# Moving the loads of one batch to a later point of the GpSimd queue, and a batch's sums ahead of a group of h, in a fused convolution and mixer kernel

## Chip, cores and metric

The kernel runs on one core of a Trainium2 chip. The metric is the device time of one execution in microseconds; the time of a kernel is the median of several runs. A change of under about 1% is hard to tell from no change with it.

## What is computed

The input x has 8 batches of 4224 tokens with 192 channels, in float32. First comes a causal convolution with 7 taps; each of 8 heads (24 channels each) has its own taps, which are softmaxed. Its result, here called y, goes through a mixer: a low-rank mix over the tokens (rank 32) gives h, and then come two matrix products over the channels with a ReLU between them.

```python
w = softmax(weight, axis=-1)                       # 8 heads x 7 taps
out = np.einsum('hk,bskhg->bshg', w, x_unf)        # causal windows of 7 tokens
x = out.reshape(B, S, D)                           # this is y below
xt = x.transpose(0, 2, 1)
h = xt @ U @ V                                     # U: 4224x32, V: 32x4224
u = x + h.transpose(0, 2, 1)
ch = np.maximum(u @ w_ch1, 0.0) @ w_ch2            # 192 -> 768 -> 192
return (u + ch).astype(np.float32)
```

## The kernel before

**Tiles and groups.** A tile is 128 tokens. A batch has 33 tiles, and the 264 tiles of all batches are taken in 33 groups of 8, so that a group may lie across two batches.

**Convolution.** The x of a batch is loaded into `x_sb` (two buffers, so that batches b and b + 2 share one), as bf16, in blocks of 64 tokens on half of the partitions each. `x_part` (L76) is one load of a part of it, issued on the GpSimd (POOL) queue; the list `XP` (L84) has the four parts of a batch: two of 384 KB, one of 432 KB and one of 408 KB. From batch 2 on, the convolution (`conv32`, matmuls at L340, results moved to `y_sb` at L272 on ScalarE and at L274 on VectorE) also needs `xb_sb`, a rearranged copy of `x_sb` with a single buffer. `x_shift` (L299) makes it with four GpSimd copies: L303, L304 and twice L316. Between these copies it also loads the batch that comes next: after L304 it clears the halo of the next `x_sb` (L74) and issues the first two parts, and after the copies of L316 the other two, all at L79. The condition for that, `more`, is in L308.

**Mixer.** The sum of y times U over the tokens of a batch is `tt_mm` (33 matmuls at L399). `tt_split` takes it out of PSUM as a high part (ScalarE, L413) and a low part (VectorE, L414), and `tt_sum` adds these up with two matmuls at L455 and writes `tt_sb` (VectorE, L449). For a group g, `h_group` multiplies `tt_sb` by V (8 matmuls at L484) and adds y on VectorE (L506), which gives `u_sb`. `transp` (L523) has SP issue a DMA transpose of `u_sb` to `uT` (L525). `w1` multiplies `uT` by W1 (36 matmuls of 512 columns at L578, six blocks m of six) and applies the ReLU on ScalarE (L589) or VectorE (L591). `w2` multiplies that by W2 for two tiles at a time (12 matmuls at L602), VectorE adds u (L610, tile `out_sb`, eight buffers), and SP issues the store (L617). The transposes and the stores share one hardware DMA queue; the loads of x go through the software queue that GpSimd serves. PSUM has eight banks, given out in turn by `bank()`.

**Order.** The schedule is manual: every engine executes its instructions in the order in which the program emits them, and the order is written out by hand in `SLOTS` (L630). A slot first does W1 of its groups and then W2 of its groups, with four places p per group; at a place, other work is put in ahead of W2: `h` and a number is `h_group` and `transp` of that group, `c` a piece of the convolution (batch, first head, number of heads, engines that move it out), `x` is `x_shift`, `t` is `tt_mm` and `tt_split`, and `s` is `tt_sum`. The slots that matter here:

- slot 2: W1 of group 2, W2 of group 1; at place 4 h of group 4 and `x2`
- slot 3: W1 of group 3, W2 of group 2; at place 1 h of group 5
- slot 4: W1 of groups 4 and 5 one after the other, W2 of groups 3, 4 and 5; at places 0, 4, 7 and 10 h of groups 6, 7, 8 and 9, at places 1 to 3 the convolution of batch 2, and at place 3 `x3` behind it
- slot 5: W1 and W2 of groups 6 to 8; the convolution of batch 3 begins at place 3, and `x4` is at place 7
- slots 6 to 9 (k = 6 to 9 in the loop of L651): W1 and W2 of three groups each; the convolution of batch b = k - 2 at places 4, 5 and 8, with `x{b+1}` behind its last piece, the third h of the slot and `t{b}` at place 10, and `s{b}` at place 12, behind the slot's last W2

**Held loads.** For batch 2 alone, `LOADS` (L682) puts the loads elsewhere: each of the four parts is emitted behind the W1 of a group and waits for the end of one of its six blocks (`held`, L619; the pair (2, 5) is the last block of W1 of group 2). The loop at L737 does this for every batch that `LOADS` names.

Of the kernel before, what the change touches and what calls it, by code (L numbers as in the profile page):

```python
# [14 lines left out]
def kernel(  # L15
# [12 lines left out]
    B, S, D = x.shape  # L28
# [33 lines left out]
    xt = [None] * B  # L62
# [7 lines left out]
    def x_tile(b):  # L70
        xt[b] = xs.tile([P, NB1 + 1, D], BF16, name="x_sb")

    def x_zero(b, eng):
        eng.memzero(xt[b][0:HB, 0, :])  # L74

    def x_part(b, r, s0, s1):  # L76

        blk = NB0 * r + s0 - 1
        return nc.gpsimd.dma_start(  # L79
            out=xt[b][HB * r : HB * r + HB, s0:s1, :],  # L80
            in_=x[b, blk * HB : (blk + s1 - s0) * HB, :].rearrange("(j p) d -> p j d", p=HB),
        )

    XP = [(0, 1, 17), (0, 17, NB0 + 1), (1, 0, 18), (1, 18, NB1 + 1)]  # L84
# [214 lines left out]
    def x_shift(b):  # L299


        xbt[b] = xbs.tile([P, NB1, D], BF16, name="xb_sb")
        nc.gpsimd.tensor_copy(out=xbt[b][:, 0:NB0, :], in_=xt[b][:, 1 : NB0 + 1, :])  # L303
        nc.gpsimd.tensor_copy(  # L304
            out=xbt[b][HB : HB + QB, NB0:NB1, :],
            in_=xt[b][HB : HB + QB, NB0 + 1 : NB1 + 1, :],
        )
        more = XP if b + 1 < B and xt[b + 1] is None else []  # L308
        if more:
            x_tile(b + 1)  # L310
            x_zero(b + 1, nc.gpsimd)
        for xp in more[:2]:
            x_part(b + 1, *xp)
        for r in range(2):
            q = slice(HB * r + QB, HB * r + HB)
            nc.gpsimd.tensor_copy(  # L316
                out=xbt[b][q, 0 : (NB0, NB1)[r], :], in_=xt[b][q, 0 : (NB0, NB1)[r], :]
            )
        for xp in more[2:]:
            x_part(b + 1, *xp)  # L320
# [249 lines left out]
    def w1(g, pat):  # L570
        rl = rls.tile([P, MC, 2, 4 * P], BF16, name="rl_sb")
        rlt[g] = rl
        ends = []
        for m in range(MC):
            pp = [bank(), bank()]
            for c in range(3):
                for hf in range(2):
                    last = nc.tensor.matmul(  # L578
                        out=pp[hf][:],
                        lhsT=W1_sb[HB * hf : HB * hf + HB, c, m * P : (m + 1) * P],  # L580
                        rhs=uTt[g][HB * hf : HB * hf + HB, :, c, :],
                        start=(c == 0),
                        stop=(c == 2),
                        tile_position=(HB * hf, 0),
                    )
            ends.append(last)
            for hf in range(2):
                if pat[m][hf] == "A":
                    nc.scalar.activation(out=rl[:, m, hf, :], in_=pp[hf][:], func=ACT.Relu)  # L589
                else:  # L590
                    nc.vector.tensor_scalar_max(out=rl[:, m, hf, :], in0=pp[hf][:], scalar1=0.0)  # L591
        return ends
# [58 lines left out]
    for k in range(5, 14):  # L651
        gs = list(range(3 * k - 9, 3 * k - 6))
        hs = [f"h{g}" for g in range(nh, min(nh + 3, NG))] + [None] * 3
        nh = min(nh + 3, NG)
        if k == 5:
            at = {
                0: [hs[0]],
                3: ["c3:0:3:A"],
                4: ["c3:3:2:AAD"],
                5: [hs[1]],  # L660
                7: ["c3:5:3:AD", "x4"],
                9: ["t3"],
                10: ["s3"],
                11: [hs[2]],
            }
        elif k < 10:
            b = k - 2
            at = {
                0: [hs[0]],
                4: [f"c{b}:0:3:AAD"],  # L670
                5: [f"c{b}:3:3:AAD"],
                6: [hs[1]],
                8: [f"c{b}:6:2:AD"] + ([f"x{b + 1}"] if b + 1 < B else []),
                10: [hs[2], f"t{b}"],
                12: [f"s{b}"],
            }
        else:
            at = {0: [hs[0]], 4: [hs[1]], 8: [hs[2]]}
        SLOTS.append((gs, gs, {p: [w for w in what if w] for p, what in at.items()}))
    assert nh == NG  # L680

    LOADS = {2: [(1, 5), (1, 5), (2, 2), (2, 5)]}  # L682


    idle(30, P)
# [27 lines left out]
    def do(what):  # L713
        if what[0] == "c":
            b, h0, n, engs = what[1:].split(":")
            conv32(int(b), int(h0), int(n), engs)
            return
        if what[0] == "d":
            for h in range(H):
                conv(int(what[1:]), h, 1, [0, 1], "AD")  # L720
            return
        n = int(what[1:])
        if what[0] == "h":
            h_group(n)
            if n > 1:
                transp(n)
        elif what[0] == "x":
            x_shift(n)
        elif what[0] == "t":
            tt_split(n, tt_mm(n, range(NT)))  # L730
        else:
            tt_sum(n)

    for gs1, gs2, at in SLOTS:
        for g in gs1:
            ends = w1(g, RELU0 if g < 2 else RELU)
            for b, blocks in LOADS.items():  # L737
                for q, (gb, m) in enumerate(blocks):
# [49 lines left out]
```

## Time and profile before

| | |
|---|---|
| median of 5 runs | 336.06 us (333.69 to 337.11) |
| time of the profiled execution | 336.06 us |
| its span, from the first to the last instruction | 334.3 us |
| mean granted TensorE clock | 0.992 |
| busy PE / DVE / ACT / POOL | 319.9 / 274.9 / 166.6 / 139.3 us |
| DMA: software queue (loads of x) / hardware queue (stores, transposes) | 14.73 / 38.18 MB |

The profiled execution lay at the median, and its time is 1.8 us above its span. PE is the TensorE matmul, PEld the weight load beside it, DVE is VectorE, ACT ScalarE, POOL GpSimd, and SP the engine that issues the stores and transposes. Times in the rows are microseconds from the start of the span, and a number behind a line number in a row ("x36") counts instructions. In a row of waits the last three figures are the sum in microseconds, how often, and the longest. "Landing" is the time from the start of the issue of a DMA to its completion.

### The profile page before, as it was taken

Reading aid. Unit: us, or ns where it says so; the run is one execution under the profiler, and the core shown is the slowest. Engines: PE = TensorE matmul, PEld = TensorE weight load, DVE = VectorE, ACT = ScalarE, POOL = GpSimd, SP = SyncE. Lnnn points to the kernel's source line nnn. Section 1 sums busy time; section 2 is a strip of 40 time slices with the busy share of each in tenths; the row PEclk is TensorE's granted clock in tenths of the full one; section 3 lists DMA queues with packets and bytes.
Section 4 is the critical chain, followed back from the end, with each engine's and each line's share of the span. In section 5 each row is a group of like instructions: output and inputs, shape, how many; then the busy total and the mean of one; then the engine's idle time right before and its main releaser. Section 6 shows DMA issues by size and latency. Waiting matters only on the chain.

```text
span 334.3 us, 9715 instructions
## 1 busy us (share of the span) xinstructions
PE 319.9 (96%) x4072; PEld 218.3 (65%) x4072; DVE 274.9 (82%) x558; ACT 166.6 (50%) x340; POOL 139.3 (42%) x91
## 2 busy tenths in 40 slices
PE   6889999789999999999999998999999999999994
PEld 6645676447747846764874784587487487487494
DVE  5746998779988898998898869889798898896863
ACT  1648454463295184558429535842921921912910
POOL 8580217964990796299289529700000000000000
PEclk9989999999999999999999999999999999999998
DMA  8999995969999996998999699077149349249045
GB/s 102 192 166 139 169 212 143 159 121 218 194 220 183 253 148 86 261 202 122 130 288 184 79 248 229 2 190 187 53 82 247 100 111 226 91 109 259 14 129 157
DMA packets 122909, 53.55 MB, mean 160 GB/s; under 512 B 87760, under 2 KB 122832, under 8 KB 122864
## 3 DMA queue, kind: packets, MB, share of 16 engines
q1 hardware_dynamic: 84672, 38.18, 50.1%
q0 software_dynamic: 38192, 14.73, 39.0%
q8 instruction: 32, 0.52, 0.6%
q14 instruction: 13, 0.11, 0.1%
HBM read 29.49 MB, written 25.95 MB: 166 GB/s over the span
## 4 chain that ended last, share of the span: by engine, by line
PE 86%; DMA 5%; DVE 4%; ACT 2%; issue 1%; POOL 0%; SPq 0%; DVEq 0%; POOLq 0%
PE ps L602 39%; PE ps L578 37%; PE ps L340 3%; DMA x_sb<-in_x_dram 3%; PE ps L484 3%; DMA uT<-u_sb 2%; PE ps L399 2%; DVE y_sb L274 2%; ACT y_sb L272 1%; DVE u_sb L506 1%; ACT rl_sb L589 1%; DVE rl_sb L591 1%; PE ps L536 0%; PE ps L369 0%; PE ps L455 0%
## 5 line engine op out<-in xcount | busy, mean ns | idle before, releaser
L589 ACT ACTIVATE rl_sb<-ps 128x512 bf16<-128x512 f32 x235 | 125.4, 603 | 89.2 <-PE ps L578 85.8
L602 PE MATMUL ps<-W_sb,rl_sb 128*128 128x192 bf16 x1584 | 140.5, 246 | 0.8 <-DVE out_sb L610 0.6
L578 PE MATMUL ps<-uT,W_sb 64*128 64x512 bf16 x1188 | 133.4, 380 | 3.6 <-DMA uT<-u_sb 2.9
L602 PEld LDWEIGHTS <-rl_sb 128*128 128x128 bf16 x1584 | 128.3, 98 | 12.1 <-issue 11.5
L591 DVE TENSOR_SCALAR rl_sb<-ps 128x512 bf16<-128x512 f32 x161 | 105.8, 690 | 26.1 <-PE ps L578 25.4
L578 PEld LDWEIGHTS <-W_sb 64*128 64x128 bf16 x1188 | 58.3, 95 | 75.5 <-issue 7.0
L610 DVE TENSOR_TENSOR out_sb<-ps,u_sb 128x384 f32<-128x384 f32 (+1 forms) x133 | 70.0, 550 | 19.5 <-PE ps L602 18.5
L506 DVE TENSOR_TENSOR u_sb<-y_sb,ps 128x192 bf16<-128x192 bf16 (+1 forms) x168 | 66.3, 462 | 0.0
L316 POOL COPY xb_sb<-x_sb 32x6144 bf16<-32x6144 bf16 (+1 forms) x12 | 65.5, 5460 | 0.6
L303 POOL COPY xb_sb<-x_sb 128x6144 bf16<-128x6144 bf16 x6 | 31.8, 5302 | 52.8 <-PE ps L340 27.5
L272 ACT ACTIVATE y_sb<-ps 128x384 bf16<-128x384 f32 (+3 forms) x79 | 32.3, 502 | 36.4 <-PE ps L340 34.6
L79 POOL DMA_DIRECT2D x_sb<-in_x_dram x32 | 27.0, 853 | 17.3 <-PE ps L484 9.6
L274 DVE CAST y_sb<-ps 128x408 bf16<-128x408 f32 (+2 forms) x53 | 26.6, 554 | 2.5 <-PE ps L369 2.5
L484 PE MATMUL ps<-tt_sb,V_sb 32*128 32x192 bf16 x264 | 13.2, 247 | 0.3 <-DVE y_sb L274 0.2
L340 PE MATMUL ps<-xb_sb,band 64*32 64x384 bf16 x192 | 12.4, 332 | 0.1
L340 PE MATMUL ps<-x_sb,band 64*32 64x384 bf16 x192 | 12.1, 332 | 0.0
L484 PEld LDWEIGHTS <-V_sb 32*128 32x128 bf16 x264 | 4.9, 92 | 9.5 <-issue 9.5
L413 ACT ACTIVATE tt_hi<-ps 128x192 bf16<-128x192 f32 x7 | 2.3, 331 | 15.9 <-PE ps L399 15.9
L173 PE MATMUL ps<-zz 128*128 128x128 bf16 x90 | 7.1, 254 | 1.2 <-DVE zz L168 1.2
L173 PEld LDWEIGHTS <-zz 128*128 128x128 bf16 x90 | 6.8, 117 | 1.2 <-DVE zz L168 1.2
L369 PE MATMUL ps<-x_sb,band 64*64 64x312 bf16 (+3 forms) x192 | 7.2, 277 | 0.4 <-DMA x_sb<-in_x_dram 0.4
L340 PEld LDWEIGHTS <-band 64*32 64x32 bf16 x384 | 4.4, 89 | 4.5 <-issue 3.0
(64 smaller groups left out, 71.7 us busy)
## 6 DMA issues: line engine op xcount, KB each, us to landing
out_dram<-out_sb SPq DMA_DIRECT2D x131, 192.0 KB, 3.0
x_sb<-in_x_dram POOLq DMA_DIRECT2D x14, 384.0 KB, 8.0
x_sb<-in_x_dram POOLq DMA_DIRECT2D x7, 432.0 KB, 6.5
x_sb<-in_x_dram POOLq DMA_DIRECT2D x7, 408.0 KB, 8.6
x_sb<-in_x_dram POOLq DMA_DIRECT2D x1, 648.0 KB, 9.7
x_sb<-in_x_dram POOLq DMA_DIRECT2D x1, 624.0 KB, 7.2
uT<-u_sb SPq DMA_TRANSPOSE x31, 5.3
W_sb<-in_moe_w_ch_dram POOLq DMA_DIRECT2D x2, 192.0 KB, 5.8
```

Of the source, the lines that this page charges most:

```text
L272: nc.scalar.activation(out=out, in_=in_, func=ACT.Copy)
L274: nc.vector.tensor_copy(out=out, in_=in_)
L303: nc.gpsimd.tensor_copy(out=xbt[b][:, 0:NB0, :], in_=xt[b][:, 1 : NB0 + 1, :])
L316: nc.gpsimd.tensor_copy(out=xbt[b][q, 0 : (NB0, NB1)[r], :], in_=xt[b][q, 0 : (NB0, NB1)[r], :])
L340: nc.tensor.matmul(out=pp[r][QB * cg : QB * cg + QB, 0 : nk[r] * GS], lhsT=w[hr], rhs=t[hr, st : st + 2 * nk[r] - 1 : 2, hs], start=True, ...
L484: nc.tensor.matmul(out=banks[pr][:, a * D : (a + 1) * D], lhsT=V_sb[32 * q : 32 * q + 32, (j // 8) * 2 + j % 2, :], rhs=ttb[b][32 * q : 32 ...
L506: nc.vector.tensor_tensor(out=u_group(g)[:, i : i + n, :, hf, :], in0=yt[b][:, run[0] : run[0] + n, :].rearrange("p n (c k) -> p n c k", c=3),
L578: last = nc.tensor.matmul(out=pp[hf][:], lhsT=W1_sb[HB * hf : HB * hf + HB, c, m * P : (m + 1) * P], rhs=uTt[g][HB * hf : HB * hf + HB, :, ...
L589: nc.scalar.activation(out=rl[:, m, hf, :], in_=pp[hf][:], func=ACT.Relu)
L591: nc.vector.tensor_scalar_max(out=rl[:, m, hf, :], in0=pp[hf][:], scalar1=0.0)
L602: nc.tensor.matmul(out=cps[:, a * D : (a + 1) * D], lhsT=rlt[g][:, m, hf, (i + a) * P : (i + a + 1) * P], rhs=W2_sb[:, m, :], start=(m == ...
L610: nc.vector.tensor_tensor(out=o[:, 0:n, :].rearrange("p n (c k) -> p n c k", c=3), in0=cps[:, 0 : n * D].rearrange("p (n c k) -> p n c k", ...
```

## The change

Three lines change. With the first, `x_shift(2)` no longer loads batch 3; `x_shift` of batches 3 to 6 loads the next batch as before. With the third, the four loads of batch 3 are emitted behind W1 of groups 4 and 5 and wait for the blocks 1 and 4 of each. On the GpSimd queue they so stand behind all the copies of `x2`, and ahead of those of `x3`; the clearing of the halo goes with the first. With the second, `t{b}` is emitted ahead of the third h at place 10 of slots 6 to 9 (batches 4 to 7), on every engine.

```diff
@@ -305,7 +305,7 @@
             out=xbt[b][HB : HB + QB, NB0:NB1, :],
             in_=xt[b][HB : HB + QB, NB0 + 1 : NB1 + 1, :],
         )
-        more = XP if b + 1 < B and xt[b + 1] is None else []
+        more = XP if 2 < b < B - 1 else []
         if more:
             x_tile(b + 1)
             x_zero(b + 1, nc.gpsimd)
@@ -671,7 +671,7 @@
                 5: [f"c{b}:3:3:AAD"],
                 6: [hs[1]],
                 8: [f"c{b}:6:2:AD"] + ([f"x{b + 1}"] if b + 1 < B else []),
-                10: [hs[2], f"t{b}"],
+                10: [f"t{b}", hs[2]],
                 12: [f"s{b}"],
             }
         else:
@@ -679,7 +679,7 @@
-    LOADS = {2: [(1, 5), (1, 5), (2, 2), (2, 5)]}
+    LOADS = {2: [(1, 5), (1, 5), (2, 2), (2, 5)], 3: [(4, 1), (4, 4), (5, 1), (5, 4)]}
```

## The prediction

> **What bounds it now.** I read the page's busy times first, then TensorE's own waits, then the chain of work that ended last. TensorE is the bound, and what it can still give is small.
>
> ```profile
> PE 319.9 (96%) x4072; PEld 218.3 (65%) x4072; DVE 274.9 (82%) x558; ACT 166.6 (50%) x340; POOL 139.3 (42%) x91
> ```
>
> The waits of TensorE name two that this change touches: one for a transpose and one for the low part of a batch's sum, with a wait for VectorE's `out_sb` just ahead of the latter.
>
> ```profile
> PE ps L578 <- DMA uT<-u_sb: 2.9, 1, 2.9
> PE ps L455 <- DVE tt_lo L414: 1.0, 1, 1.0
> PE ps L602 <- DVE out_sb L610: 0.6, 1, 0.6
> ```
>
> In the chain the first stands as a transfer of 7.45 us between h and W1 of group 5 (W1 of group 4 had ended at 64.75, so TensorE stood for 2.9):
>
> ```profile
> 58.90 1.09 DVE u_sb L506 x3
> ...
> 60.14 7.45 DMA uT<-u_sb
> ...
> 67.64 4.06 PE ps L578 x36
> ```
>
> Why is this transpose slow? The DMA view of two stretches of its life (packets, MB, share) answers: first from 61 to 65 us, then from 65 to 67.6. q0 carries the loads of x, q1 transposes and stores.
>
> ```profile
> q0 software_dynamic: 1761, 0.67, 148.1%
> q1 hardware_dynamic: 11, 0.00, 0.5%
> ```
>
> ```profile
> q1 hardware_dynamic: 1845, 0.60, 107.1%
> q0 software_dynamic: 186, 0.07, 21.5%
> ```
>
> The transpose moves nothing until the two loads of batch 3, issued just ahead of it, are through (the second landed at 66.5). GpSimd's timeline shows these loads (L79 at 58.26) and what stands around them:
>
> ```profile
> 52.22 5.30 POOL L303 COPY xb_sb<-x_sb 128x6144 bf16<-128x6144 bf16 x1 [8.12 <-DMA x_sb<-in_x_dram]
> 57.58 0.50 POOL L304 COPY xb_sb<-x_sb 32x384 bf16<-32x384 bf16 x1
> 58.14 0.17 POOL L74 MEMSET x_sb<- 64x96 uint32 x1
> 58.26 1.63 POOL L79 DMA_DIRECT2D x_sb<-in_x_dram  x2
> 59.93 10.98 POOL L316 COPY xb_sb<-x_sb 32x6144 bf16<-32x6144 bf16 x2
> 70.86 1.72 POOL L79 DMA_DIRECT2D x_sb<-in_x_dram  x2
> 79.83 5.30 POOL L303 COPY xb_sb<-x_sb 128x6144 bf16<-128x6144 bf16 x1 [7.25 <-DMA x_sb<-in_x_dram]
> ...
> 87.54 10.98 POOL L316 COPY xb_sb<-x_sb 32x6144 bf16<-32x6144 bf16 x2
> ```
>
> **Part 1, the loads: what is removed.** Without the loads, the transpose of 60.14 has the DMA engines to itself. The transpose at 226.12, with no load near, landed after 3.7 us; that at 54.23, also without one, after 5.3. So it lands between 63.8 and 65.5, against a W1 of group 5 that can begin at 64.75: TensorE gains 2.1 to 2.9. I take 2.9, since nine of the eleven transposes behind 210 us, where there are no loads left, took 4.0 or less.
>
> **Part 1: what moves.** On the POOL queue the halo and two issues leave the middle of batch 2's copies, so L316 starts at 58.1 and ends at 69.1 instead of 70.9. The convolution of batch 2, which needs them, began at 73.26 and would now begin at 70.4: 1.3 us of room, no cost. Then come the halo and four issues at 0.85 each (1.63 and 1.72 a pair), the first at 69.3, the last at 71.8. Their added waits, for blocks 1 and 4 of W1 of groups 4 and 5, cost nothing: a block takes 11.76 / 18 = 0.65 us (the chain's W1 of three groups), and block 4 of group 5 ends near 68.1. Even if the transpose stayed late, it would end at 70.9, ahead of the fourth issue. Behind these on POOL stand only the copies of batch 3, which have to wait for the landing anyway. SP's queue is not reordered, but its stores and transposes now meet these loads.
>
> **When do they land?** Before, two parts issued at 70.86 let L303 start at 79.83, 8.97 later. Now two parts of 384 KB more are in the same string, 2048 packets. From 23 to 29 us the loads of batch 1 ran alone at 2998 packets in 6 us, or 500 per us; from 61 to 65 it was 1761 in 4 us, or 440. So they add 4.1 to 4.7 us, and L303 of batch 3 starts at 69.3 + 8.97 + 4.1 to 4.7 = 82.4 to 83.0. A second way: the four loads of batch 1, issued together from 18.81, had the last landed at 32.43, 13.6 later: 82.9. L303 so starts some 3 us later than before.
>
> **What is late next.** From L303 to the end of the second L316 it is 98.52 - 79.83 = 18.7 us, whatever else happens. The convolution of batch 3 began at 104.19; with the 2.9 gained TensorE asks for it at 101.3. L303 must then start by 101.3 - 18.8 = 82.5. This is the narrow place of the change: each microsecond later than 82.5 is taken off the gain, and at 85.4 it is gone.
>
> **Rule against row.** The group 6 transpose (issued at 74.59, now near 71.7) falls into the string of four loads. At 60.14 and 131.83, with loads issued about 2 us ahead, the loads went through first. The Trainium skill, DMA: Bandwidth & Descriptors, "Queues, rings and completion order", says otherwise: each DMA engine alternates between the queues that have work, packet by packet. Then the loads would be slowed by everything on q1: a transpose of some 2.2 us (65.4 to 67.6) and the four stores of the first places of W2, 0.5 each by the spacing of their landings: 4.2. L303 would start at 86.6 to 87.2 and the convolution of batch 3 at 105.7, 1.5 later than before: a loss instead of a gain. The row says 0 to 0.6 of the 2.9 is lost. Sharing is seen where the transpose came before the loads or within 1.2 us of them (issued at 85.83: its loads took 8.7 and 11.4 to land). I stay near the row, with 0.5 for a little sharing: L303 at 83.1, the convolution at 101.9, **gain 2.3** (ends: -1.5 and 2.9).
>
> Behind it the chain recovers: loads of batch 4 issued 3.3 later end near 110.5 against a convolution of batch 3 that ends near 108.3, so the POOL copies of batch 4 start about as before (110.77), and the convolution of batch 4 has 4.2 us of room (129.5 to 133.56), 1.9 after the gain. But the second pair of batch 4's loads (98.47, now near 101.8) comes to lie on the transpose of group 10 (103.48, now 101.2). Such a meeting at 187.06 and 188.04 made the stores late, and TensorE lost 0.6 + 1.0; at 158.76 and 159.91 nothing. **I take -0.3** (0 to -1.7).
>
> **Part 2, the order of t and h.** VectorE's timeline at the one place where the low part was late:
>
> ```profile
> 200.53 0.56 DVE L610 TENSOR_TENSOR out_sb<-ps,u_sb 128x384 f32<-128x384 f32 x1 [1.70 <-PE ps L602]
> 201.01 2.07 DVE L506 TENSOR_TENSOR u_sb<-y_sb,ps 128x192 bf16<-128x192 bf16 x6
> 202.99 0.35 DVE L414 TENSOR_TENSOR tt_lo<-ps,tt_hi 128x192 bf16<-128x192 f32 x1
> 203.26 1.01 DVE L610 TENSOR_TENSOR out_sb<-ps,u_sb 128x384 f32<-128x384 f32 x2
> ```
>
> The stores were behind (the wait of 1.70 can only be for a free `out_sb`, as W2 had long ended), and six adds of h stood ahead of the low part. With the new order it runs at 201.0, and the 1.0 goes; the 0.6 stays. Given back: W1's first ReLU on VectorE now follows W1's start by about 2.3 us instead of 0.9; the banks of W2's last pair and of the sum come free near 204.3 and 204.8, and W1's fourth block, which needs them, begins at 202.4 + 3 x 0.65 = 204.4: 0.35 is lost. **Net 0.65** (0 to 1.0). At the other three places TensorE did not wait for the low part. There VectorE will idle 0.65 (the row at 113.96, where no h stands between, waits that long for the high part), its ReLUs come 0.75 later, and PSUM has about 0.2 to 0.3 to spare; I take 0 (0 to -0.3 each). The h moved back is for a W1 a whole slot later, some 28 us.
>
> **Sum.** 2.3 - 0.3 + 0.65 = 2.65 from the profiled execution's 336.06, which is also the median: **333.4**.
>
> **Rivals.** (a) All of it comes: 2.9 + 1.0 = 3.9, so 332.2. For it: the loads of batch 1 and a landing at 82.4. Against: the four loads have never met a transpose. (b) The loads share the DMA engines, and the copies of batch 3 become the bound. The meeting at 187.06 had its pair landed 11.4 after the first issue, the quiet pair at 70.86 took 8.8; at twice the difference, 5.2, for two pairs, L303 starts at 87.9 and the convolution of batch 3 at 106.7, 2.5 later than before; with part 2's 0.65 that is 337.9. It decides against the change from L303 at 86.1 on. Against it is the row at 60.14. (c) Group 5's transpose is no earlier, because the stores or its own work held it, or another stall takes the gain at once: 336. Against it: 11 packets in 4 us.
>
> **How the numbers follow.** Forecast 0.52 (333.4, by itself 332.3 to 334.8), (a) 0.20, (b) 0.19, (c) 0.09. About 1% is what a measurement of this kernel can tell from no change: 332.7 and 339.4. Below 332.7 lie most of (a) and a tenth of the forecast, 0.26; above 339.4 somewhat under half of (b), 0.09, where L303 starts past 89.4; the rest is 0.65. The range reaches from (a) to (b), 331.6 to 338.2.
>
> **What would show it.** Right: no wait of L578 for `uT` near 65 us; L79 four times from 69.3 on; L303 of batch 3 near 83; no idle of TensorE ahead of L340 near 102; no wait of L455. Wrong: a TensorE wait for `xb_sb` there or for group 6's `uT` near 86; new waits for `out_sb`; POOL standing in L79 on W1.

## The result, and the profile after

The changed kernel is slower: 339.34 us median of 43 runs against 336.72 of 80 runs of the kernel before, ratio 1.0092 (95% interval 1.0071 to 1.0114). The ratio compares fast runs alone, those at most 1.5% above the fastest of their kernel, and comes to 3.1 us of loss; the medians differ by 2.6. A gain of 2.65 us was forecast. The runs of either kernel spread over more than 7 us, and the profiled execution of the changed kernel was one of its fastest: 335.83 us, span 334.1. A second profile of it (the tenth experiment) has a span of 339.4. The spans can't be set directly against that of before, since the profiled execution of before lost 1.4 us at its start (TensorE's clock was at half from 22.0 to 25.4 us), where the change can't matter. So I compare stage by stage.

The page of the changed kernel has TensorE as the bound as before:

```profile
PE 321.3 (96%) x4072; PEld 221.3 (66%) x4072; DVE 274.0 (82%) x558; ACT 166.5 (50%) x340; POOL 139.5 (42%) x91
```

The waits of TensorE on the changed kernel, in the first profile and then in the second:

```profile
PE ps L340 <- POOL xb_sb L316: 2.8, 1, 2.8
...
PE ps L578 <- DVE out_sb L610: 0.2, 1, 0.2
PE ps L602 <- DVE out_sb L610: 0.2, 1, 0.2
```

```profile
PE ps L340 <- POOL xb_sb L316: 4.6, 2, 2.6
PE ps L578 <- DVE out_sb L610: 1.2, 2, 0.8
...
PE ps L602 <- DVE out_sb L610: 0.8, 2, 0.6
```

The wait for the transpose of group 5 (2.9) and that for the low part of the sum (1.0) are gone. VectorE's timeline has the low part ahead of the adds of h, right behind the store wait:

```profile
201.63 0.56 DVE L610 TENSOR_TENSOR out_sb<-ps,u_sb 128x384 f32<-128x384 f32 x1 [1.23 <-DMA out_dram<-out_sb]
202.10 0.35 DVE L414 TENSOR_TENSOR tt_lo<-ps,tt_hi 128x192 bf16<-128x192 f32 x1
202.37 2.06 DVE L506 TENSOR_TENSOR u_sb<-y_sb,ps 128x192 bf16<-128x192 bf16 x6
```

A wait for the copies of batch 3 stands in the place of the two, and in the second profile another one at batch 5. GpSimd's timeline of the changed kernel shows where it comes from:

```profile
56.44 10.98 POOL L316 COPY xb_sb<-x_sb 32x6144 bf16<-32x6144 bf16 x2
67.48 0.17 POOL L74 MEMSET x_sb<- 64x96 uint32 x1
67.60 3.35 POOL L79 DMA_DIRECT2D x_sb<-in_x_dram  x4
85.42 5.30 POOL L303 COPY xb_sb<-x_sb 128x6144 bf16<-128x6144 bf16 x1 [14.47 <-DMA x_sb<-in_x_dram]
...
93.15 10.98 POOL L316 COPY xb_sb<-x_sb 32x6144 bf16<-32x6144 bf16 x2
```

The four loads are issued where they should be, but L303 starts 17.8 us after the first of them, not 13.8. The views of the DMA issues give the fourth load 15.2 us to land and the transpose of group 6, issued at 70.08, 12.2. Three stretches of the DMA view tell why, first 71 to 74 us, then 75 to 79, then 79.6 to 80.8 (q0 carries the loads, q1 transposes and stores):

```profile
q0 software_dynamic: 1391, 0.53, 152.6%
```

```profile
q0 software_dynamic: 1122, 0.42, 85.2%
q1 hardware_dynamic: 1104, 0.28, 53.4%
```

```profile
q1 hardware_dynamic: 71, 0.02, 82.0%
q0 software_dynamic: 71, 0.03, 61.5%
```

Up to 74.5 the loads have the engines to themselves, at 464 packets per us. Then the transpose begins, and the two queues move as many packets each: 1122 against 1104. The loads go on at 280 per us. By these rates, five microseconds of sharing cost the loads about 2.0 of the 4.0 us, an estimate. The third stretch is close to a standstill of both queues, for about 1.2 us. The second profile and several experiments have it as well, and the fourth experiment, without this transpose, does not (500 packets in the same stretch); its cause isn't shown. From 81 on the loads share with the stores.

The chain of the changed kernel, in the stretch that follows:

```profile
74.37 10.04 DMA out_dram<-out_sb
...
84.53 0.56 DVE out_sb L610
...
93.15 5.29 POOL xb_sb L316
98.44 0.06 issue
98.50 5.63 POOL xb_sb L316
104.14 0.04 issue
104.18 0.71 PE ps L340 x17
```

A store behind that transpose takes 10 us, VectorE has no free `out_sb` until it lands, and further on the chain lies on GpSimd's copies. From the first W1 of slot 5 to that of slot 6 it is 28.2 us before (89.0 to 117.2) and 34.2 after (84.5 to 118.7). The gain up to slot 5 was made: from W1 of group 4 to W1 of group 6 it is 28.3 before (60.7 to 89.0) and 25.3 after (59.3 to 84.5). The loss of 6.0 in slot 5 is more than the wait of 2.8. W1 of groups 6 to 8 ends 13.3 us after its start instead of 11.8, for want of banks behind the late stores: 1.5. The wait behind it is shorter by as much, since the copies end when they end. And the granted clock, in the view of windows (the column behind the five engines' busy times), falls behind the wait:

```profile
101.00:104.20 3.20, 0.43 (x10) 0.11 (x8) 0.78 (x2) 0.00 (x0) 3.20 (x2) 1.00 1.16 211
104.20:105.00 0.80, 0.80 (x26) 0.43 (x26) 0.00 (x0) 0.41 (x2) 0.80 (x2) 1.00 1.09 365
105.00:108.50 3.50, 3.50 (x35) 2.42 (x34) 1.11 (x2) 3.32 (x9) 0.81 (x1) 0.51 1.14 153
108.50:112.00 3.50, 3.50 (x63) 2.70 (x61) 2.86 (x7) 0.22 (x2) 0.00 (x0) 1.00 1.45 222
```

For 3.4 us of the stretch from 105.0 to 108.5 the clock is at half, which is worth 1.7 us. 2.8 + 1.5 + 1.7 = 6.0, against 3.0 gained: at the start of slot 6 the changed kernel is 2.9 us late. This is not yet the loss of the whole execution. Slot 8, where the profile of before had its waits of 0.6 and 1.0, takes 28.4 us instead of 30.0, so that from W1 of group 4 to the last W1 this execution loses 1.4 us. The second profile loses 6.8: 3.7 up to the start of slot 6, the rest behind it, above all in slot 7 (32.1 us instead of 28.2). That the first profile is 2.9 late at slot 6 and the runs lose 3.1 is a coincidence.

Could the loss be nothing but executions with more half-clock stretches? Of the changed kernel's 44 runs, 18 had a mean clock from 0.9925 to 0.997, median 337.3 us, and 22 a lower one, 341.1. Of the 43 runs of the kernel before that ran beside the fifteenth experiment, 23 lay in the same band, median 336.1, and 13 below it, 337.7. So the loss is there at equal clock too, and low clocks are somewhat more frequent besides.

### The profile page after: what moved, and what is told of

It reads as the page before. It is cut to its first block, busy times and chain, and to the rows that moved or that the text cites. A ratio compares the mean times of both kernels' runs of the same rounds, so it can differ in the third digit from the quotient of the medians.

```text
span 334.1 us, 9716 instructions
## 1 busy us (share of the span) xinstructions
PE 321.3 (96%) x4072; PEld 221.3 (66%) x4072; DVE 274.0 (82%) x558; ACT 166.5 (50%) x340; POOL 139.5 (42%) x91
## 4 chain that ended last, share of the span: by engine, by line
PE 75%; DMA 9%; POOL 6%; DVE 5%; ACT 3%; issue 1%; DVEq 0%; POOLq 0%
PE ps L602 34%; PE ps L578 34%; DMA out_dram<-out_sb 6%; POOL xb_sb L316 3%; DMA x_sb<-in_x_dram 3%; ACT rl_sb L589 2%; PE ps L484 2%; PE ps L340 2%; DVE y_sb L274 2%; POOL x_sb L79 1%; PE ps L399 1%; DVE rl_sb L591 1%; DVE out_sb L610 1%; DVE u_sb L506 1%; DMA V_sb<-in_moe_V_dram 1%
## 5 line engine op out<-in xcount | busy, mean ns | idle before, releaser
L602 PEld LDWEIGHTS <-rl_sb 128*128 128x128 bf16 x1584 | 129.2, 98 | 12.1 <-issue 11.4
L578 PEld LDWEIGHTS <-W_sb 64*128 64x128 bf16 x1188 | 59.7, 94 | 69.9 <-issue 6.5
L610 DVE TENSOR_TENSOR out_sb<-ps,u_sb 128x384 f32<-128x384 f32 (+1 forms) x133 | 69.8, 550 | 25.4 <-PE ps L602 21.6
L303 POOL COPY xb_sb<-x_sb 128x6144 bf16<-128x6144 bf16 x6 | 31.8, 5302 | 55.8 <-DMA x_sb<-in_x_dram 32.3
L340 PE MATMUL ps<-xb_sb,band 64*32 64x384 bf16 (+1 forms) x192 | 13.1, 340 | 2.9 <-POOL xb_sb L316 2.8
```

What stands on the lines that cost most here:

```text
L340: nc.tensor.matmul(out=pp[r][QB * cg : QB * cg + QB, 0 : nk[r] * GS], lhsT=w[hr], rhs=t[hr, st : st + 2 * nk[r] - 1 : 2, hs], start=True, ...
L578: last = nc.tensor.matmul(out=pp[hf][:], lhsT=W1_sb[HB * hf : HB * hf + HB, c, m * P : (m + 1) * P], rhs=uTt[g][HB * hf : HB * hf + HB, :, ...
L602: nc.tensor.matmul(out=cps[:, a * D : (a + 1) * D], lhsT=rlt[g][:, m, hf, (i + a) * P : (i + a + 1) * P], rhs=W2_sb[:, m, :], start=(m == ...
L610: nc.vector.tensor_tensor(out=o[:, 0:n, :].rearrange("p n (c k) -> p n c k", c=3), in0=cps[:, 0 : n * D].rearrange("p (n c k) -> p n c k", ...
```

## The experiments

Fifteen kernels were run, and the changed kernel once more. Theory 1: the loss is in the string of four loads that meets the transpose of group 6. Its first rivals: the new order of t and h costs (theory 2 of the first two expectations); any later load only moves the collision (rival 3); four loads in a string are slow by themselves (rival 4). From the eleventh experiment on, theory 2 is a new one, given before it. Ratios are to the kernel before, with 95% intervals.

### Each part alone

The first experiment has the changed lines 308 and 682 alone, the second line 674 alone.

> The loads of batch 3 moved, the order of t and h as before. Theory 1 (the loss lies in the moved loads: four loads in one string meet the transpose of group 6, the DMA engines are shared, the copies of batch 3 end late and the stores fall behind): 0.6 to 1.2% slower, about what the whole change gave; TensorE waits about 2 to 4 us for xb_sb ahead of the convolution of batch 3, and L303 of batch 3 starts some 17 to 18 us after the first of the four loads. Theory 2 (the loss lies in the new order of t and h, which makes VectorE's ReLUs late): faster by 0 to 0.7%.

> The sums of a batch ahead of h, the loads as before. Theory 1 (the loss lies in the moved loads): within 0.3% of before, at most 0.3% faster, and no TensorE wait of L455 for the low part at any of the four places. Theory 2 (the new order makes VectorE's ReLUs late): 0.6 to 1.2% slower, with TensorE waiting for banks in the W1 behind each of the four sums.

Loads alone: 1.0168 (1.0126 to 1.021). Order alone: 0.9987 (0.9963 to 1.0012). The loss is in the loads, and larger than the 0.6 to 1.2% expected; theory 2 of these two falls. The two ratios don't multiply to the 1.0092 of the whole change: beside the moved loads the new order seems worth more than by itself, which was not followed up. With the loads alone TensorE waited 3.7 us for the copies, and L303 started 18.6 us after the first load. With the order alone the wait of L455 is not in the profile, which leaves the one for the transpose:

```profile
PE ps L578 <- DMA uT<-u_sb: 3.4, 1, 3.4
```

### Another place for the first pair

Third experiment, from the kernel before:

```diff
-        for xp in more[:2]:
+        for xp in more[:2] if b > 2 else []:
             x_part(b + 1, *xp)
         for r in range(2):
             ...
+            for xp in more[:2] if (b, r) == (2, 0) else []:
+                x_part(b + 1, *xp)
```

> As before, but the first pair of batch 3's loads is issued between the two copies of L316, some 5.5 us later than before and behind the issue of the transpose of group 5; the second pair stays behind the second copy. Theory 1 (the gain at group 5 is real, and it was lost since all four loads went into one string with the transpose of group 6): the transpose of group 5 lands in 3.7 to 4.5 us, TensorE does not wait for it, the copies of batch 3 end before TensorE asks, and the kernel is 0.5 to 0.9% faster. Rival 3 (any later load of batch 3 makes later transfers collide and gives the gain back): within 0.3% of before.

The transpose of group 5 landed in 3.65 us and TensorE did not wait for it. But eight of nine runs took 336.7 to 340.3 us and one 329.6, so that no ratio is given; faster it is not, and as a forecast of theory 1 this missed. The profile shows four waits for `xb_sb`, 6.0 us in all. The transpose of group 6 came earlier with the gain, at 69.96, and so between the issues of the second pair (69.37 and 70.20), whose last part took 13.3 us to land. The collision had moved, as rival 3 has it.

### The transpose left out

Fourth experiment, from the whole change:

```diff
-            if n > 1:
+            if n == 6:
+                uTt[n] = uTt[n - 1]
+            elif n > 1:
                 transp(n)
```

> The whole change, but the transpose of group 6 is left out, and W1 of group 6 reads the transposed tile of group 5 instead; everything else is done. Theory 1 (the transpose shares the DMA engines with the four loads): the loads run alone for longer and L303 of batch 3 starts 2 to 3 us sooner than with the whole change, 15 to 15.5 us after the first load (what is left of sharing is with the stores), TensorE's wait for xb_sb falls to about 0 to 1 us, and the stores are no longer late; 0.7 to 1.2% faster than the whole change, about level with before. Rival 4 (four loads in a string are slow by themselves, by the descriptors or the memory): L303 starts no sooner than 17 us after the first load, and the time stays within 0.3% of the whole change.

Ratio 1.0005 (0.9982 to 1.0029): level with before, as theory 1 expected, but not by its path. L303 still started 16.6 us after the first load (15 to 15.5 was expected, 17 or more by rival 4), as the next transpose and the stores took the left-out one's share, and TensorE still waited for the copies:

```profile
PE ps L340 <- POOL xb_sb L316: 3.4, 1, 3.4
```

Slot 5 took 34.2 us as with the whole change, and the four slots behind it 28.0 to 28.3 each. So the traffic of the other queue matters, not this one transpose; and what the profiles have to tell this kernel from the second one of the whole change lies in the slots behind slot 5. Rival 4 gets no support: the four loads of batch 1, with nothing on the other queue until the last of them was through, landed in 13.6 us, and the string takes longer where other traffic meets it.

### The transpose of group 6 later

In these four h of group 6 stands at place 2 of slot 4 instead of place 0:

```diff
-                0: ["h6"],
                 1: ["c2:0:3:AAD"],
-                2: ["c2:3:3:AD"],
+                2: ["c2:3:3:AD", "h6"],
```

> The first pair of batch 3's loads between the copies of L316, as in the third experiment, and h of group 6 with its transpose moved from place 0 to place 2 of slot 4, so that the transpose is issued some 3 to 4 us after the second pair. Theory 1 (a transpose or store issued close to a pair shares the DMA engines with it; one issued 3 us later does not): the second pair lands as in the kernel before, L303 of batch 3 starts 9 to 9.5 us after that pair's first issue (14.3 in the third experiment), no TensorE wait for xb_sb there, and 0.6 to 1% faster than before. Rival 3 (moving these loads only moves the collision): L303 on time, but a TensorE wait for xb_sb or uT of a microsecond or more at batch 4 or later, and within 0.3% of before or slower.

> The kernel of the fifth experiment with the sums of a batch ahead of h as well. Theory 1: 0.1 to 0.4% faster than the fifth, so 0.7 to 1.3% faster than before. Rival 3: within 0.3% of before or slower, as the fifth.

> A control: the kernel before with h of group 6 and its transpose at place 2 instead of 0. Theory 1 (the later transpose matters only beside the moved loads): within 0.3% of before; TensorE still waits 2.9 us for the transpose of group 5. Rival (the place of this h is worth something by itself): more than 0.4% either way.

> The whole change with h of group 6 and its transpose at place 2 instead of 0, 2 to 3 us behind the issue of the last of the four loads. Theory 1 in the form that what is issued first goes first: the transpose moves nothing until the loads are nearly through, some 6 us or more after its issue; only the two stores ahead of it share, L303 of batch 3 starts 14 to 15 us after the first load (17.8 with the whole change), and the kernel is 0.5 to 1.2% faster than the whole change. Theory 1 in the form that a transfer on the other queue starts some 4.4 us after its issue at the latest and then shares equally: L303 15.5 to 16.5 us after the first load, 0.2 to 0.6% faster than the whole change. Rival 4 (four loads in a string are slow by themselves): 17 us or more, no faster than the whole change.

Fifth (on the third): 0.9888 (0.9812 to 0.9964). Sixth (with the new order as well): 0.9892 (0.9863 to 0.9922). Seventh (the kernel before): 1.0006 (0.9974 to 1.0037). The gain at group 5 can be had, 1.1%. The last part of the second pair took 7.65 us to land, and L303 started 8.6 us after that pair's first issue. GpSimd's timeline of the sixth, for comparison with the one above:

```profile
62.61 1.63 POOL L79 DMA_DIRECT2D x_sb<-in_x_dram  x2
64.28 5.62 POOL L316 COPY xb_sb<-x_sb 32x6528 bf16<-32x6528 bf16 x1
69.85 1.72 POOL L79 DMA_DIRECT2D x_sb<-in_x_dram  x2
78.84 5.30 POOL L303 COPY xb_sb<-x_sb 128x6144 bf16<-128x6144 bf16 x1 [7.28 <-DMA x_sb<-in_x_dram]
```

L303 starts at 78.8 against 85.4, with TensorE at the same point: rival 3 falls for this placement.

Eighth (the whole change with the later transpose): 1.0172 (1.0111 to 1.0233). L303 came 16.6 us after the first load, just past the 15.5 to 16.5 of the second form of theory 1: a transpose issued 3.6 us behind the last load still shared with them from 80 us on. "What is issued first goes first" falls. The time was no better, against both forms; TensorE waited three times for `xb_sb`, at batches 3, 4 and 6 (2.9, 2.2 and 1.1).

### Is the wait at batch 3 the loss?

Ninth, from the whole change, and the tenth, which is the whole change again:

```diff
-        for r in range(2):
+        for r in range(2) if b != 3 else [1]:
             q = slice(HB * r + QB, HB * r + HB)
             nc.gpsimd.tensor_copy(
```

> The whole change, but the first of the two L316 copies of batch 3 is left out, so a quarter of that batch's rearranged copy holds the wrong rows; nothing else differs. GpSimd reaches the end of batch 3's copies 5.3 us sooner while all loads, transposes and stores are as in the whole change. Theory 1 (what the change loses is TensorE's wait behind the late copies of batch 3, and what follows from it): no TensorE wait for xb_sb at batch 3, and the time falls to 0.5 to 1.2% below before, as in the sixth experiment. Rival 5 (the loss is in the stores and transposes that come late in the four loads, or in later batches, whatever the copies do): no faster than before, with waits of TensorE for out_sb or uT in slots 4 and 5 in the place of the one for xb_sb.

> The whole change once more, for a second profile beside the ninth experiment. Theory 1: 0.7 to 1.1% slower than before; TensorE waits 2.5 us or more for xb_sb ahead of the convolution of batch 3, L303 of batch 3 starts 17 to 19 us after the first of the four loads, and in the slower executions one of batches 4 to 7 shows a second wait for xb_sb or for the stores. Rival 5: the wait for xb_sb is below 1.5 us and others take its place.

Ninth: 1.0071 (1.0007 to 1.0134). Tenth: 1.0077 (1.0031 to 1.0122). With the wait at batch 3 taken away the median came no lower, and theory 1 in this narrow form misses. The edit did more than expected, though. Slot 5 shrank to 31.2 us, but the second pair of batch 4 was now issued at 102.06, before its first pair had landed (105.70) and 0.4 us behind a transpose; it took 14.4 us to land, and L303 of batch 4 started at 116.64 instead of 112.86. So the ninth shows that what is won at batch 3 can be lost again at the next batch, not that the wait cost nothing. The waits of the ninth are at batches 4 and 6 (3.1 and 3.0), and those for banks in W1 are larger than in the first profile:

```profile
PE ps L340 <- POOL xb_sb L316: 6.1, 2, 3.1
...
PE ps L578 <- DVE out_sb L610: 1.7, 2, 1.3
```

This gave a new theory (theory 2 from here on): GpSimd's cycle as a whole falls behind. From L303 of a batch to the issue of the second pair of the next it is 18.6 us, then 8 to 14 us pass until that pair has landed, and then comes the next L303; TensorE's slot takes 28.2. With 9 us to land the cycle takes 27.8, with 14 us 32.8. In the tenth L303 stands at these places, 28 to 33 us apart, each right behind the landing of the last load of its batch (at 114.67, 147.86 and 175.78 for the last three), whichever engine the row names:

```profile
86.17 5.30 POOL L303 COPY xb_sb<-x_sb 128x6144 bf16<-128x6144 bf16 x1 [14.89 <-DMA x_sb<-in_x_dram]
...
114.87 5.30 POOL L303 COPY xb_sb<-x_sb 128x6144 bf16<-128x6144 bf16 x1 [8.30 <-PE ps L602]
...
148.01 5.30 POOL L303 COPY xb_sb<-x_sb 128x6144 bf16<-128x6144 bf16 x1 [12.74 <-PE ps L602]
...
175.97 5.30 POOL L303 COPY xb_sb<-x_sb 128x6144 bf16<-128x6144 bf16 x1 [7.56 <-PE ps L602]
```

### GpSimd late in the kernel before, and wider spacing

Eleventh, from the kernel before, and twelfth, from the sixth:

```diff
+        for _ in range(2 if b == 3 else 1):
-        nc.gpsimd.tensor_copy(out=xbt[b][:, 0:NB0, :], in_=xt[b][:, 1 : NB0 + 1, :])
+            nc.gpsimd.tensor_copy(out=xbt[b][:, 0:NB0, :], in_=xt[b][:, 1 : NB0 + 1, :])
```

```diff
-                0: [hs[0]],
+                1: [hs[0]],
                 4: [f"c{b}:0:3:AAD"],
```

> The kernel before, with the first copy (L303) of batch 3 done twice, so that GpSimd runs 5.3 us late from there on; the loads of batch 3 and the order are those of before, and the copies of batch 3 then end just about where TensorE asks for them (98.5 + 5.3 = 103.8 against 104.2). Theory 2, new (what costs is that GpSimd's cycle of copies and loads falls behind TensorE's: the second pair of a batch's loads is then issued beside a transpose, shares the DMA engines with it, and the next batches are late as well): 0.4 to 1.2% slower than before, with TensorE waits for xb_sb of 2 us or more at batch 4 or later, and a second pair of batch 4 that takes 11 us or more. The narrow form of theory 1 (only TensorE's wait at batch 3 itself costs): at most 0.2% slower.

> The kernel of the sixth experiment, and in slots 6 to 9 the first h and its transpose at place 1 instead of 0, so that this transpose is issued 2 us instead of 1 us behind a batch's second pair of loads. Theory 2: the second pairs of batches 5 to 7 land within 9 us of their first issue in place of 9 to 11, no waits for stores in slot 8, and the kernel is 0 to 0.4% faster than the sixth experiment, 1.1 to 1.5% faster than before. Rival (these meetings cost nothing any more once GpSimd keeps pace): within 0.2% of the sixth experiment.

Eleventh: 1.0038 (1.0009 to 1.0067), slower, but at the low end of the 0.4 to 1.2% that the new theory expected, and its profile has none of the expected waits for `xb_sb`: the second pairs landed in 8.7 to 9.4 us, so that the cycle just kept pace. In this profile, being late was not enough; the pairs must be slow to land as well. Twelfth: 0.9885 (0.9862 to 0.9908), the fastest median of all at 331.62 us. Its interval covers the sixth, so the wider spacing shows no gain of its own. The second pairs of batches 5 to 7 took 9.1 to 9.9 us from the first issue to the last landing, above the 9 expected and no less than in the sixth (8.2 to 9.5).

### What the wait does to the clock

Thirteenth, from the whole change, with `i28` a call of `idle(28, P)`, and fourteenth, from the kernel before:

```diff
-                3: ["c3:0:3:A"],
+                3: ["i28", "c3:0:3:A"],
```

```diff
+            if g == 5:
+                idle(28, P)
             ends = w1(g, RELU0 if g < 2 else RELU)
```

> The whole change, with 28 matmuls of zeros (some 2.2 us, into a bank that nobody reads) ahead of the convolution of batch 3, so that TensorE works in most of the time in which it waits there for the copies. Theory 3 (a TensorE wait of 2 us or more costs more than its length, since the granted clock drops to half for 3.4 us behind it, worth some 1.7 us): the half-speed stretch near 105 us is gone, slot 5 takes 32.5 us or less in place of 34.2, and the kernel is 0.3 to 0.6% faster than the whole change, some 0.4 to 0.6% slower than before. Rival 6 (the wait costs its length and no more; the clock is a matter of chance): within 0.2% of the whole change, or slower by what the matmuls take where the copies are early.

> The kernel before, with the same 28 matmuls of zeros between W1 of group 4 and W1 of group 5, where TensorE waits 2.9 us for the transpose. Theory 3: no half-speed stretch near 67 to 70 us in any profile, and 0.1 to 0.4% faster than before, since that stretch was there in some executions (seen in the seventh and eleventh experiments, not in the profile of before). Rival 6: within 0.1% of before.

Thirteenth: 1.0179 (1.013 to 1.0227), slower than the whole change where 0.3 to 0.6% faster was expected. Fourteenth: 1.0 (0.9965 to 1.0034). In the profile of the thirteenth TensorE is kept at work and the clock stays up:

```profile
101.00:104.60 3.60, 2.69 (x40) 2.34 (x38) 1.49 (x4) 0.00 (x0) 3.60 (x2) 1.00 1.38 183
104.60:108.10 3.50, 3.48 (x71) 2.40 (x70) 1.12 (x3) 3.07 (x9) 1.64 (x2) 1.00 1.20 274
```

Slot 5 took 33.0 us instead of 34.2, somewhat short of the expected 32.5. That fits a half clock that comes from the wait, worth 1.2 there. One profile can't settle it: the eighth and the ninth have waits of 2.9 and 3.1 us with the clock up. And the whole time was worse: slots 6 and 7 took 29.7 and 32.0 (28.2 each in the first profile), with new waits for `xb_sb` at batches 4 and 5. What TensorE gains at batch 3 it loses behind it. At the old wait the filling made no difference to the median, so that part of theory 3 isn't shown.

### A shorter cycle for all batches

Fifteenth (from the whole change) and sixteenth (from the kernel before):

```diff
-        for r in range(2):
+        for r in range(2) if b < 3 else [1]:
```

> The whole change, with the first of the two L316 copies left out for every batch from 3 on (a quarter of each rearranged copy holds the wrong rows), so that GpSimd's cycle of copies and loads is 5.3 us shorter for each of these batches; all loads, transposes and stores remain. Theory 2 (from batch 3 on the change is bound by GpSimd's cycle: 18.7 us of copies and issues and 9 to 14 us for the second pair to land, against 28.2 us for a slot of TensorE): no TensorE wait for xb_sb at any batch from 3 on, and 0.6 to 1.3% faster than before, while the ninth experiment, which shortened batch 3 alone, was 0.7% slower. Rival 5 (the loss is in late stores and transposes, whatever the copies do): no faster than before.

> The control: the kernel before with the same copies left out. Theory 2 (before, GpSimd kept pace with TensorE): within 0.4% of before, so that the fifteenth is faster than this one by the 0.5 to 1% that the transpose of group 5 is worth. Rival (the kernel before was bound by GpSimd's cycle as well): more than 0.6% faster than before.

Fifteenth: 0.9949 (0.9924 to 0.9974). Sixteenth: 0.9975 (0.994 to 1.001). With GpSimd's cycle 5.3 us shorter at every batch from 3 on, the changed kernel goes from 0.9% slower to 0.5% faster, just short of the expected 0.6; no wait for `xb_sb` is left, though its four loads were as slow as ever (L303 of batch 3 at 87.29, 17.8 after the first) and the stores as late. What is left behind them are waits for banks:

```profile
PE ps L578 <- DVE out_sb L610: 0.9, 2, 0.6
```

Slot 5 took 30.2 us, so that about 2.0 us of the loss there are the stores' and stay. Rival 5 (the loss is in late stores and transposes, whatever the copies do) falls for the whole, and the kernel before was not bound by this cycle in the same way. The fifteenth was to be 0.5 to 1% faster than its control; it is so by 0.3%, and the intervals overlap, so that the gain at group 5 isn't shown by this pair.

## Why the prediction was wrong, step by step

- **TensorE's gain at group 5**: right. The transpose landed in 3.67 us, and 3.0 us were gained up to slot 5, against the 2.9 taken.
- **Batch 2's copies and the waits for W1**: right. The copies ended at 67.4, no wait for them is in the profile, and the four issues follow each other without a gap.
- **"The row says 0 to 0.6 of the 2.9 is lost ... I stay near the row, with 0.5 for a little sharing: L303 at 83.1"**: this step failed. It came to 13.8 us after the first load; the runs of the change show 17.8 and 18.3. The row that I leaned on (11 packets on q1 in 4 us) was misread. The transpose of 60.14 moved its first packet at 64.5, 4.4 us after its issue, when the two loads were nearly through. In the changed kernel it is 4.4 us again (70.08 and 74.5), but now two loads are left. What looked like precedence was a late start. The Trainium skill's rule (DMA: Bandwidth & Descriptors, "Queues, rings and completion order") that the queues alternate packet by packet fits the 1122 against 1104 packets; its sum, 86.6 to 87.2 or 17.3 to 17.9 us after the first load, came out right, though in part by luck: it has neither the late start of the transpose nor the standstill near 80.
- **What is late next**: the price was right up to the start of batch 3's convolution. With the 1.4 us of the start added, L303 came at 86.9 on the clock of the profile of before, 4.4 past the 82.5, which takes the gain of 2.9 to a loss of 1.5; the convolution began at 105.6, 1.4 later than before. (The late stores cost nothing on top of this, as they only shorten the wait.) What the prediction put at nothing is what the wait does next: 1.7 us of half clock, which brings the lateness to 2.9 at slot 6. The Trainium skill's TensorE: Matmul & The Clock Gate, "Part 1: The HAM clock gate", tells that an idle window of about 3.4 us halves the clock. The trace agrees with the half and the length (0.50, 3.4 us), and has it behind waits of 2.0 and 2.8, shorter than that window.
- **"Behind it the chain recovers"**: failed in the slower executions. The room at batch 4 (4.1 us by the rows, 129.46 to 133.56; the prediction has 4.2) was enough in the first profile, but GpSimd's cycle had about 0.4 us to spare per batch (28.2 less 27.8), and a pair that met a transpose used up far more. The second profile has a half-speed stretch and a wait of 2.0 at batch 5, and slot 7 took 32.1 us.
- **Part 2, 0.65**: the mechanism is right (no wait of L455 in any profile with the new order), the size is not shown: 0.13% or 0.4 us, with an interval that holds nothing as well as the 0.65. Of the eight profiles with the old order six have the wait, 0.6 to 1.0 us. VectorE's wait for the store ahead of it stayed, as said, and W1 behind it took 12.1 instead of 11.8.
- **Rival (b)** is what happened in kind: the copies of batch 3 became the bound. It reckoned a loss of 1.8 us by other figures (5.2 for two pairs that land late, instead of even sharing), and lacked the clock and the later batches.

What stays open: why leaving out the one transpose brought the time back although the wait of 3.4 at batch 3 remained (its profile has no later wait, but one profile doesn't show why); what decides in which later batch a pair is slow, which differs from one profile to the next; and what stops both queues near 80 us.

## What to carry to other kernels

A transfer that seems to give way to another may only have started late: look when its first packet moved, and what was left of the other then, before reckoning that a longer string will have precedence. When an engine off the critical path runs a cycle of loads and work, compare the length of that cycle with the period of the engine that bounds, for quiet and for crowded transfers: with little to spare, a delay may not be paid once but come back at later rounds, as in the profiles of the eighth, ninth, tenth and thirteenth experiments. And before moving a load away from one transfer, see what the gain itself will move into its new place.

## What the runs showed of the hardware

- In the profiles of before and after, a transpose on the hardware queue (issued with no other one under way) moved its first packet 1.2 to 1.9 us after its issue when no load was in flight, and 1.6 to 4.4 us after it when two or more software-queue loads had been issued in about the 5 us ahead of it. In the strings of four loads the two queues moved equal numbers of packets from then on. While such a transpose was under way, SP stood in the issue of the next one for up to 7.8 us (1.3 to 1.6 at most quiet places), and the stores behind it were issued that much later.
- Loads of x, converted from float32 to bf16 on the way, ran at 440 to 500 packets per us alone and at 280 beside a transpose.
- In all eighteen profiles, between 27 and 327 us, TensorE's granted clock fell to half only at waits of 2.0 to 3.7 us, for 3.4 us and in the third and fourth experiments for 6.8. Not every such wait did it: at the old wait for the transpose the clock fell in the seventh, eleventh and sixteenth experiments (3.6, 3.7 and 3.1 us) and not in the profiles of before and of the second (2.9 and 3.4).
